# A phase of its own, with seven products of quarter matrices, for the first output product

## The chip, the cores and the metric

The kernel runs on one core of a Trainium2 chip. The metric is the device time of one execution in microseconds (us), as the median of several runs.

## The reference, cut to what matters

```python
# q, k, v: (8, 8, 576, 64); attention inside chunks of 64 tokens, per head
attn = softmax(q_c @ k_c.T / 8)                    # 64 x 64 per chunk and head
x = (attn @ v_c)  ->  (4608 tokens, 512)
h = maximum(maximum(x @ w1, x @ w2), x @ w3)       # w1..w3: 512 x 768
y = h @ w_out                                      # w_out: 768 x 512, the first output product
u = maximum(y @ w_in2, 0)                          # w_in2: 512 x 2048
out = (u * u) @ w_out2                             # w_out2: 2048 x 512
```

Weights arrive as 64-bit floats for w1 to w3, w_out, w_in2 and w_out2 (512 KB for 128x512 numbers), q, k and v as 32-bit floats.

## The kernel before, in words

The 4608 tokens are 9 blocks (NB) of 512 tokens (TB); attention goes by 36 tiles of 128 tokens. Every matrix product is done with float32r operands in three terms: each operand is kept as a high part (a cast by ACT) and a low part (the rest, a subtraction by DVE), and high x high, high x low, low x high are summed in PSUM. A matmul here is always 128x128 against 128x256.

Four stages follow each other on PE. Stage 1, up to about 160 us, is a list of tokens written out by hand (`order`, lines 642 to 658, inside `tc.manual_schedule()`): attention of tiles 0 to 7 (`qk` load, `S` scores, `M`, `X`, `N`, `G` softmax steps, `T` transposes, `E`, `V` product with v, `H`, `L` high and low part of x), the 24 units that load and convert w1 to w3 and w_out (`U` load, `A C s h l` conversion on ACT, DVE, POOL, ACT, DVE), the projections of blocks 0 and 1 (`p` + block, group f, matrix w; 24 matmuls each; `ep` is what follows on ACT or DVE, `hh` and `hl` the split of h), and the first output product of block 0 (`y`, 24 matmuls per group f). `@` is one step of the attention of later tiles, `~` a piece of its softmax. Everything after the list is placed by the framework's planner, by the program's order and its own costs; each engine's queue then runs in order.

Stage 2, blocks 2 to 8 (lines 693 to 730): 18 projections a block (`p1`), the first output product (`g2`, accumulating over six groups f in four PSUM banks, one group behind the projections), one attention step per group f, and, on ACT, DVE, POOL and the DMA queue, `park`: the 8 + 8 slices of w_in2 and w_out2 are converted, combined into seven matrices per group of four and written to DRAM as high and low part (two chains of steps, `early`, 22 steps of each chain in a block). A last output y of `g2` is copied out of PSUM and written to DRAM (`y_d`).

Stage 3 (lines 736 to 775) does y @ w_in2 with seven products of half-size matrices in place of eight (`z`; 12 matmuls per product, 9 x 4 groups), which takes three ACT copies out of PSUM and DVE sums to put together; `split_y` makes the seven combinations of y and their parts. Stage 4 (lines 776 to 790) does the last product in the same way (`g4`).

All DMAs are issued by SP, in order. SBUF slots: `w` (44) and `wz` (12) tiles of 128x512, `m` (14) operands, `in` (4), `xh` and `xl` (2 each), `t` (8) temporaries. PSUM: `acc` 4 banks, `p` 2, `at` 2.

Of the kernel before, what the change touches and what calls it, by code (L numbers as in the profile page):

```python
# [31 lines left out]
NW = 44  # L32
NZ = 12
NM = 14
NG = 4
EARLY = 48

# [4 lines left out]
def kernel(ctx: ExitStack, tc, qkv, w123, w_out, w_in2, w_out2, out):  # L42
# [21 lines left out]
    def late_tile(name):  # L64
        return wp.tile([P, 512], F32R, tag="wz", name=name, bufs=NZ)

# [5 lines left out]
    zero = const.tile([P, 512 + 64 * NZ], BF16, name="zero")[:, 0:512]  # L72
# [45 lines left out]
    def unit(src, name, keep, late):  # L118


        hi, lo = [halved(late_tile(name + n) if late else wp.tile([P, 512], F32R, tag="w", name=name + n)) for n in "hl"]
# [9 lines left out]
        def A():  # L131
            if double:
                box["r"] = wp.tile([P, 512], F32, tag="w", name="r")
                box["a"] = rounded(raw, box["r"])
# [20 lines left out]
    def combine(q, left, eng):  # L155
# [3 lines left out]
        def op(name, x, y, how):  # L159
            t = tmp(name)  # L160
            eng.tensor_tensor(out=t.rearrange("p (a c) -> p a c", a=2), in0=x, in1=y, op=how)
            return t.rearrange("p (a c) -> p a c", a=2)
# [53 lines left out]
    def fetch(n, g, i, place):  # L216
        ts = []
        for j in range(2):
            if place < NZ // 2:
                t = late_tile(f"{n}{'hl'[j]}")  # L220
            else:
                t = wp.tile([P, 512], F32R, tag="w", name=f"{n}{'hl'[j]}")
            nc.sync.dma_start(t.bitcast(F32), parked[n, g][i - 1, j])
            ts.append(halved(t))
        return ts

    def operands(wide, name, early=0):
# [12 lines left out]

    def w123_unit(f, w):
        return unit(
            w123[f, :, w * 512:(w + 1) * 512], f"w{w}_{f}", lambda *t: W123.update({(f, w): t}), w == 1
        )

    def wo_unit(f):
        return unit(w_out[f * P:(f + 1) * P, :], f"wo{f}", lambda *t: WO.update({f: t}), False)
# [133 lines left out]
    def proj(wpair, xpair, name, parts=1):  # L381

        p = ps_tile("p", name)
# [12 lines left out]

    h_t, yacc, st = {}, {}, {}
    y_d = [dp.tile([P, KD, TB], F32, name=f"yd{b}") for b in range(NB)]

    def p1_end(b, f, w, p):  # L400

        if w == 0:
            st[b] = tmp("s1")
            nc.scalar.copy(st[b], p)
        elif w == 1:
            m = tmp("m1")
            nc.vector.tensor_tensor(out=m, in0=p, in1=st[b], op=ALU.max)
            st[b] = m
        else:
            h = tmp("h")  # L410
            nc.vector.tensor_tensor(out=h, in0=p, in1=st[b], op=ALU.max)  # L411
            hh, hl = h_t[b, f] = (operand("hh"), operand("hl"))
            yield
            nc.scalar.copy(hh, h)  # L414
            yield
            nc.vector.tensor_tensor(out=hl, in0=h, in1=hh.bitcast(F32), op=ALU.subtract)
        yield

    def p1(b, f, w):
        *_, p = proj(W123[f, w], x_t[b], f"p{w}")  # L420
        run(p1_end(b, f, w, p))

    def g2(b, f):
        if f == 0:
            yacc[b] = [ps_tile("acc", f"y{d}") for d in range(KD)]
        hp = h_t.pop((b, f))
        wh, wl = WO[f]
        for d in range(KD):
            a, c = d // 2, slice(d % 2 * P, d % 2 * P + P)
            mm_k(yacc[b][d], (wh[:, a, c], wl[:, a, c]), hp, f, f == 0, f == NF1 - 1)  # L430
        if f == NF1 - 1:
            for d in range(KD):
                ys = tmp("ys")
                if d % 2:
                    nc.vector.tensor_copy(ys, yacc[b][d])
                else:
                    nc.scalar.copy(ys, yacc[b][d])
                nc.sync.dma_start(y_d[b][:, d, :], ys)
            del yacc[b]

# [12 lines left out]
    def split_y(b, parts):  # L453

        ops = y_t[b] = operands(b % 2 == 0, "y", 0 if b else EARLY)
        q = [parts[k][:, :, n * HC:n * HC + HC] for k in range(2) for n in range(2)]
        for i, x in combine(q, False, nc.vector):
            split(x, *ops[i])
# [46 lines left out]
    def split_g(parts, wide, early):  # L505
# [4 lines left out]
        for i, x in combine(q, True, nc.vector):  # L510
            split(x, *ops[i])
            yield

    def g4(g, i, ops):
# [3 lines left out]
        for m in range(2):  # L518
            t = slice(m * P, m * P + P)
            for a in range(2):  # L520
                for j, (l, r) in enumerate(((gh, wh), (gh, wl), (gl, wh))):
# [3 lines left out]
                    )  # L525

# [55 lines left out]
    units = []  # L582
    for f in range(NF1):
        units += [lambda f=f, w=w: w123_unit(f, w) for w in range(3)] + [lambda f=f: wo_unit(f)]
    units[3:7] = units[4:7] + units[3:4]
# [45 lines left out]
    def item_steps(b, f, w):  # L631

        for p in proj(W123[f, w], x_t[b], f"p{w}", 2 if (b, f, w) in split_items else 1):
            yield
# [8 lines left out]
        U1 qk0 U2 U0 qk1 qk3 qk2 qk4 qk5 v0 v1 qk7 qk6 v2 v3 A1 C1 S0 s1 U5 v4 U3 M0 v5 A2 h1 C2 A0 l1  # L643
        X0 C0 S1 M1 s0 U4 v7 U6 S3 N0 X1 S2 N1 G0 M3 G1 T0 S4 M2 X3 E0 S5 N3 X2 h0 T1 N2 V0 E1 G3 M4 V1
        G2 T3 M5 X4 S7 s2 H1 H0 T2 N4 S6 E2 L0 h2 G4 X5 L1 V2 E3 l0 T4 M7 H2 V3 E4 q000 N5 H3 A5 L3 G5
        V4 L2 C5 q001 H4 A3 T5 M6 s5 U9 v6 p000 C3 X6 A4 p001 N6 U7 ep000 X7 G6 E5 N7 T6 G7 ep001 V5 E6
        l2 h5 T7 L4 s3 H5 V6 h3 p002 l3 H6 C4 E7 h4 s4 U8 p010 ep002 A6 l4 A7 L5 L6 p011 C7 A8 l5 ep010
        U11 C6 V7 p012 H7 ep011 s6 U10 h6 L7 h7 s7 A9 p100 l6 ep012 C8 p101 C9 h8 U12 ep100 hh01 s9 A10
        p102 hl01 h9 ep101 s8 hh00 l9 A11 p110 ep102 l7 C10 A12 p111 ep110 l8 U14 C12 p020 s10 ep111 h12
        C11 p112 hl00 h11 U15 U13 s12 ep020 h10 s11 p120 ep112 l10 A14 A15 C14 p021 ep120 s14 U18 h14  # L650
        A13 l14 p022 hh11 l12 ep021 C15 p030 ep022 s15 U19 U16 hh02 h15 l11 C13 y0 h13 s13 U17 ep030
        p121 l13 A16 hl02 C16 p031 ep121 h16 s16 A17 p122 ep031 hh10 hl11 A18 A19 y1 C19 l15 p130 ep122
        C18 C17 h18 p032 ep130 s18 h17 U21 U22 U20 U23 p131 s17 s19 y2 ep131 l18 ep032 l17 p132 l16 A21
        hh03 C21 p140 ep132 h21 s21 h19 l21 p141 ep140 A20 p142 ep141 p040 ep142 C20 hl10 h20 p041 s20
        hh13 ep040 l20 A23 hl03 p042 A22 ep041 y3 ep042 l19 C23 p050 @ h23 hh04 hl04 C22 p150 ep050 ~
        s22 s23 p051 ep150 ~ h22 hh12 l22 hl12 p151 @ l23 ep051 p152 ep151 p052 @ y4 ep052 ep152 hh05
        hl05 ~ y5 hh14 hh15 hl15 hl14 hl13 ~
# [4 lines left out]
    for token in order:  # L662
# [15 lines left out]
        elif kind == "y":  # L678
            g2(0, int(n))
        else:  # L680
            b, f, w = map(int, (n + "2")[:3])
# [3 lines left out]
        if token in ("S1", "V1"):  # L685
            heat(4)
        if token == "p041":
            for load in (att_load_v, att_load):
                for t in (8, 9):
                    load(t)  # L690

    first.__exit__(None, None, None)
    for f in range(NF1):
        if f not in (1, 5):
            att.pop(0)()
            soften()
            soften()
        g2(1, f)


    early = [chain.from_iterable([park(n, g) for g in range(NG)]) for n in ("wi", "wo2")]
    late = [("wi", g, i) for g in range(NG) for i in (1, 2, 5, 6, 3, 7, 4)]
    late += [("wo2", g, i) for g in range(NG) for i in (2, 1, 5, 6, 3, 7, 4)]

    def load_late(n):
        for _ in range(n):
            if late:
                w = late.pop(0)
                (WI if w[0] == "wi" else WO2)[w[1:]] = fetch(*w, (-1 - len(late)) % (7 * NG))

    pend = None
    for b in range(2, NB):
        for f in range(NF1):
            for w in range(3):
                p1(b, f, w)
                if b < NB - 1:
                    go(*early)
                    if w == 1 and f < 4:
                        go(*early)
                if w == 1 and pend:  # L720
                    g2(*pend)
                    pend = None
# [6 lines left out]
            pend = (b, f)  # L729
            if b == NB - 1 and f == 0:  # L730
                run(split_y(0, load_y(0)))
    assert not att and not todo and [next(e, None) for e in early] == [None, None]
    while late[0][:2] <= ("wi", 1):
        load_late(1)

    groups = [(b, g) for b in range(NB) for g in range(NG)]
    last = None
    more = iter(())
    for b in range(NB):
        for g in range(NG):  # L740
# [4 lines left out]
            if pend:  # L745
                g2(*pend)
                pend = None
            if last:
                bank["at"] = last[0]
                relu2(z(*last[1], 4, "at", False), *last[1], 1, 0)  # L750
                bank["at"] = a
# [9 lines left out]
            last = (a, (b, g))  # L761
# [79 lines left out]
```

## Time and profile before

| | |
|---|---|
| median of 3 runs | 1370.91 us (1370.04 to 1372.42) |
| the profiled execution | 1374.33 us, span 1372.5 us |
| PE busy | 1355.5 us, 99%, 13697 matmuls |
| DVE, ACT, POOL busy | 66%, 38%, 14% |
| granted TensorE clock, mean | 0.998 |
| DMA | 222.33 MB, 162 GB/s on the mean |

PE is TensorE's matmuls, DVE VectorE, ACT ScalarE, POOL GpSimd, SP the engine that issues the DMAs. The duration of one matmul in the rows includes its latency and overlaps with the next; the distance from start to start is the pace. A row by windows gives, for each stretch, its length and each engine's busy time in us with the number of instructions, then the granted clock as a share of full speed, the busy share of the 16 DMA engines and what they moved.

### The profile page before, as it was taken

The numbers are of one execution on the slowest core, as the hardware profiler recorded it, in microseconds if no ns is written. First come the engines' busy times: TensorE is split into PE (matmuls) and PEld (weight loads), VectorE is DVE, ScalarE is ACT, GpSimd is POOL, SyncE is SP. The second block draws the span as 40 slices with busy tenths as digits, with TensorE's granted clock in tenths as the row PEclk, the third lists the DMA queues.
The fourth block names the chain that finished last, engine by engine and source line by source line (L and its number), as shares of the span: only waits on it lengthen the run. The fifth ranks groups of instructions, "written<-read, shape, count | busy, mean of one in ns | idle before, by whom it ended". The sixth has DMA issues, their size and how long they took to land.

```text
span 1372.5 us, 32674 instructions
## 1 busy us (share of the span) xinstructions
PE 1355.5 (99%) x13697; PEld 1342.0 (98%) x13699; DVE 900.9 (66%) x1437; ACT 519.4 (38%) x904; POOL 194.4 (14%) x180
## 2 busy tenths in 40 slices
PE   7999999999999999999999999999999999999998
PEld 5999999999999999999999999999999999999998
DVE  6874665665665565623366666667667888878774
ACT  4643333343343343311233233333334444444442
POOL 3321233222422332300000000000000000000000
PEclk9999999999999999999999999999999999999999
DMA  9442454554545644617643333343598443444341
GB/s 266 134 124 85 132 165 144 204 174 146 212 145 169 230 140 161 232 49 236 192 158 120 139 139 147 139 146 138 178 353 319 151 146 126 133 142 149 129 141 45
DMA packets 101235, 222.33 MB, mean 162 GB/s; under 512 B 11232, under 2 KB 20448, under 8 KB 101088
## 3 DMA queue, kind: packets, MB, share of 16 engines
q1 hardware_dynamic: 101088, 220.25, 48.0%
q8 instruction: 107, 1.75, 0.5%
q14 instruction: 40, 0.33, 0.1%
HBM read 134.22 MB, written 85.98 MB: 160 GB/s over the span
## 4 chain that ended last, share of the span: by engine, by line
PE 86%; DVE 1%; issue 0%; POOLq 0%; POOL 0%; ACT 0%; DVEq 0%; ACTq 0%
PE z L471 25%; PE p L376 25%; PE o L522 25%; PE y L376 9%; PE X L347 1%; PE S L286 1%; PE T L319 1%; DVE pl L212 0%; DVE u L494 0%; POOL u L494 0%; POOLq L837 0%; DVE mx L293 0%; DVE sm L305 0%; DVE e L296 0%; DVE h L411 0%
## 5 line engine op out<-in xcount | busy, mean ns | idle before, releaser
L471 PE MATMUL z<-yxh,wih 128*128 128x256 f32 x560 | 154.9, 277 | 0.0
L471 PE MATMUL z<-yxh,wil 128*128 128x256 f32 x560 | 154.7, 276 | 0.0
L471 PE MATMUL z<-yxl,wih 128*128 128x256 f32 x560 | 154.7, 276 | 0.0
L522 PE MATMUL o<-wo2h,gl 128*128 128x256 f32 x504 | 139.2, 276 | 0.0
L522 PE MATMUL o<-wo2h,gh 128*128 128x256 f32 x504 | 139.2, 276 | 0.0
L522 PE MATMUL o<-wo2l,gh 128*128 128x256 f32 x504 | 139.2, 276 | 0.0
L522 PE MATMUL o<-wo2h,gxl 128*128 128x256 f32 x504 | 139.1, 276 | 0.0
L522 PE MATMUL o<-wo2l,gxh 128*128 128x256 f32 x504 | 139.1, 276 | 0.0
L522 PE MATMUL o<-wo2h,gxh 128*128 128x256 f32 x504 | 139.1, 276 | 0.0
L494 DVE TENSOR_TENSOR c<-z,s 128x512 f32<-128x512 f32 x108 | 74.2, 687 | 78.3 <-PE z L471 74.9
L414 ACT CAST hh<-h 128x512 fp32r<-128x512 f32 x54 | 33.4, 621 | 240.6 <-DVE h L411 222.5
L471 PE MATMUL z<-yh,wih 128*128 128x256 f32 x448 | 123.6, 276 | 0.0
L471 PE MATMUL z<-yl,wih 128*128 128x256 f32 x448 | 123.6, 276 | 0.0
L471 PE MATMUL z<-yh,wil 128*128 128x256 f32 x448 | 123.6, 276 | 0.0
L411 DVE TENSOR_TENSOR h<-p,m 128x512 f32<-128x512 f32 x54 | 37.1, 689 | 131.3 <-PE p L376 131.3
L494 POOL TENSOR_TENSOR u<-u,s 128x512 f32<-128x512 f32 x9 | 12.0, 1333 | 751.7 <-DVE u L494 653.2
L479 ACT COPY s<-z 128x512 f32<-128x512 f32 x108 | 63.5, 588 | 142.2 <-PE z L471 142.2
L471 PEld LDWEIGHTS z<-yxh,wih 128*128 128x128 f32 x560 | 105.1, 188 | 0.1
L471 PEld LDWEIGHTS z<-yxl,wih 128*128 128x128 f32 x560 | 105.2, 188 | 0.0
L471 PEld LDWEIGHTS z<-yxh,wil 128*128 128x128 f32 x560 | 105.1, 188 | 0.0
L522 PEld LDWEIGHTS o<-wo2l,gxh 128*128 128x128 f32 x504 | 94.6, 188 | 0.0
L522 PEld LDWEIGHTS o<-wo2h,gxl 128*128 128x128 f32 x504 | 94.6, 188 | 0.0
(184 smaller groups left out, 4056.6 us busy)
## 6 DMA issues: line engine op xcount, KB each, us to landing
gd<-g SPq DMA_DIRECT2D x144, 256.0 KB, 2.0
gr<-gd SPq DMA_DIRECT2D x72, 512.0 KB, 4.3
qk<-in_qkv SPq DMA_DIRECT2D x28, 512.0 KB, 4.2
raw<-in_w_out SPq DMA_DIRECT2D x22, 512.0 KB, 3.8
raw<-in_w SPq DMA_DIRECT2D x18, 512.0 KB, 3.9
v<-in_qkv SPq DMA_DIRECT2D x72, 128.0 KB, 5.8
yd<-ys SPq DMA_DIRECT2D x36, 256.0 KB, 3.0
yr<-yd SPq DMA_DIRECT2D x18, 512.0 KB, 5.2
```

Of the source, the lines that this page charges most:

```text
L286: nc.tensor.matmul(s_t[t][o:o + D, h ^ t % 2, :], lhsT=q[r, h, :], rhs=k[r, h, :], start=True, stop=True,)
L319: nc.tensor.transpose(tp[:, p * P:(p + 1) * P], e[:, 2 * p:2 * p + 2, :].rearrange("p h k -> p (h k)"), ident)
L347: nc.tensor.matmul(xps_t[t][j * D:j * D + D, p, c * D:c * D + D], lhsT=v[o:o + D, c, p, :], rhs=et[o:o + D, p, q:q + D], start=True, stop= ...
L376: nc.tensor.matmul(dst[:, c], lhsT=lhs, rhs=rhs[:, c], start=first and i == 0 and j == 0, stop=last and j == len(pairs) - 1, skip_group_ch ...
L411: nc.vector.tensor_tensor(out=h, in0=p, in1=st[b], op=ALU.max)
L414: nc.scalar.copy(hh, h)
L471: nc.tensor.matmul(dst[:, a * HC:a * HC + HC], lhsT=l[:, a, w], rhs=r[:, k, :], start=first and a + k + j == 0, stop=j == 2, skip_group_ch ...
L479: nc.scalar.copy(t, bank[tag])
L494: (eng or nc.vector).tensor_tensor(out=t, in0=x, in1=y, op=ALU.add)
L522: nc.tensor.matmul(bank[i][:, m * HC:m * HC + HC], lhsT=l[:, a, t], rhs=r[:, a, :], start=g + m + a + j == 0, stop=g == NG - 1 and j == 2, ...
```

## The change

The first output product leaves stages 1 and 2 and becomes a phase between stage 2 and stage 3. h (768 features x 512 tokens) and w_out (768 x 512) are cut into quarters (384 x 256 each), and seven products of combinations of quarters replace the eight. What each part does:

- `p1_end` no longer splits h. It writes h's quarters to DRAM (`h_d`), and for every second group f forms four differences of quarters with DVE (`t`, `u`, each 128x256) and writes them too: seven matrices per block.
- `park_wo`, first in the chain of w_in2, converts w_out, combines its quarters on POOL and writes seven matrices (high and low parts, three tiles each) to DRAM. The six w_out units leave stage 1.
- `load_h`, `split_h` and `yq` are the new phase: load the seven h matrices of the next block, split them (two casts on ACT, two subtractions on DVE for each), multiply (18 matmuls per product), and put the results together with three sums on DVE and four copies on ACT, as in stage 3. `last` is product 4 of the block before; `pull` fetches one weight matrix of w_in2 (nine in blocks 0 and 1 together), two in block 8.
- Projections of stage 2 use the four `acc` banks (in stage 1 those with f > 0), the hand-written order of stage 1 is a new one, without `y`, `hh`, `hl`; `c` stands for the differences of h. 28 steps of each preparation chain go into a block. The attention steps that stood in block 1's output product (lines 693 to 698) are `@` tokens now, seven in all.
- `w` has 56 slots, `wz` is gone; stage 3 and 4 exchange which blocks use the wide operands.

```diff
 def p1_end(b, f, w, p):
@@ w == 2
-            h = tmp("h")
-            nc.vector.tensor_tensor(out=h, in0=p, in1=st[b], op=ALU.max)
-            hh, hl = h_t[b, f] = (operand("hh"), operand("hl"))
-            yield
-            nc.scalar.copy(hh, h)
-            yield
-            nc.vector.tensor_tensor(out=hl, in0=h, in1=hh.bitcast(F32), op=ALU.subtract)
+            h = weight("h", F32)
+            nc.vector.tensor_tensor(out=h, in0=p, in1=st[b, f], op=ALU.max)
+            h = halved(h)
+            j = f // 2
+            if f % 2 == 0:
+                nc.sync.dma_start(h_d[b][0, :, j, :], h[:, 0, :])
+                h_t[b, j] = h
+            else:
+                nc.sync.dma_start(h_d[b][1:5:3, :, j, :].rearrange("i p n -> p i n"), h)
+                yield
+                q = h_t.pop((b, j))
+                t, u = [halved(weight(n, F32)) for n in "tu"]
+                for out, x, y in (
+                    (t[:, 0], q[:, 1], q[:, 0]), (t[:, 1], h[:, 1], t[:, 0]),
+                    (u[:, 0], h[:, 1], q[:, 1]), (u[:, 1], h[:, 0], t[:, 1]),
+                ):
+                    nc.vector.tensor_tensor(out=out, in0=x, in1=y, op=ALU.subtract)
+                for k, x in ((2, t), (5, u)):
+                    nc.sync.dma_start(h_d[b][k:k + 2, :, j, :].rearrange("i p n -> p i n"), x)
...
-    def g2(b, f):
...
+    def load_h(b, part):
+        if part == 0:
+            pairs, one = ((0,) if b == 0 else (0, 2)), ((2, 3, 4, 5) if b == 0 else ())
+        else:
+            pairs, one = (), ((6,) if b == 0 else (4, 5, 6))
...
+    def split_h(b):
+        for k, i in enumerate(QN):
+            if i in (3, 4):
+                t = ap.tile([P, KD, TB], F32R, tag="xl", name=f"h{i}").rearrange("p k n -> p (k n)")
...
+            else:
+                ts = [operand("h" + n) for n in "hlm"]
...
+            for h, y in zip(hi, xs):
+                nc.scalar.copy(h, y)
+            for h, l, y in zip(hi, lo, xs):
+                nc.vector.tensor_tensor(out=l, in0=y, in1=h.bitcast(F32), op=ALU.subtract)
+            yield
+    def yq(b, i, tag, first):
...
+        for a in range(2):
+            c = slice(a * P, a * P + P)
+            for j in range(NJ):
+                for k, (l, r) in enumerate(((wh, hh), (wh, hl), (wl, hh))):
+                    nc.tensor.matmul(
+                        dst[:, a * HC:a * HC + HC], lhsT=l[j][:, c], rhs=r[j],
+                        start=first and a + j + k == 0, stop=k == 2, skip_group_check=True,
+                    )
...
@@ order, its last lines
+        l11 h13 U16 U15 C14 U17 p122 ep121 s14 s13 p130 s12 A16 h12 C16 p031 l12 h16 s16 h14 ep130 p131
+        A15 ep031 l13 ep122 l14 p032 C15 h15 s15 A17 p040 C17 ep131 p041 s17 ep040 ep032 h17 c01 p132
+        ep041 l17 l15 p042 ep132 c11 l16 p050 @ ep042 p051 ~ ~ ep050 p052 @ @ ep051 p140 ~ ep052 c02
+        p141 @ ep140 p142 ~ ep141 p150 @ @ p151 ~ ep150 p152 @ ~ ep151 ep142 ep152 c12
...
-    for f in range(NF1):
-        if f not in (1, 5):
-            att.pop(0)()
...
-        g2(1, f)
...
-    early = [chain.from_iterable([park(n, g) for g in range(NG)]) for n in ("wi", "wo2")]
+    early = [
+        chain(park_wo(), *[park("wi", g) for g in range(NG)]), chain(*[park("wo2", g) for g in range(NG)])
+    ]
...
                 if b < NB - 1:
                     go(*early)
-                    if w == 1 and f < 4:
+                    if w and f < 5:
                         go(*early)
...
+            if b == NB - 1:
+                if f == 0:
+                    load_h(0, 0)
+                    more = split_h(0)
+                else:
+                    next(more)
...
+    for b in range(NB):
+        if b + 1 < NB:
+            load_h(b + 1, 0)
+        yq(b, 1, "at", True)
+        a, s1 = bank["at"], take("at", "s1")
+        next(more)
+        pull(b)
+        c11 = plus(yq(b, 2, "p", True), s1, "c11")
+        put_y(b, 0, 0, c11)
+        if last:
+            last()
+        bank["at"] = a
+        next(more)
+        pull(b)
+        if b + 1 < NB:
+            load_h(b + 1, 1)
+            more = split_h(b + 1)
+        else:
+            more = split_y(0, load_y(0))
+        yq(b, 5, "acc", True)
+        s5 = take("acc", "s5")
+        next(more)
+        pull(b)
+        yq(b, 6, "at", False)
...
```

## Rows read from the trace of the kernel before

**Rows 1.** Page: busy us, share of the span, instructions.
```profile
PE 1355.5 (99%) x13697; PEld 1342.0 (98%) x13699; DVE 900.9 (66%) x1437; ACT 519.4 (38%) x904; POOL 194.4 (14%) x180
```
**Rows 2.** Windows: stretch, its length, each engine's busy us, clock, DMA share, GB/s.
```profile
0.00:10.00 10.00, 5.18 (x43) 2.42 (x43) 3.92 (x8) 3.96 (x6) 1.97 (x7) 1.00 0.79 278
10.00:20.00 10.00, 8.04 (x170) 6.78 (x172) 9.32 (x19) 3.81 (x8) 3.36 (x3) 0.83 1.06 301
20.00:30.00 10.00, 7.24 (x125) 5.60 (x125) 8.45 (x18) 3.52 (x7) 4.36 (x4) 0.83 1.06 239
...
60.00:80.00 20.00, 20.00 (x179) 20.00 (x178) 16.61 (x26) 11.14 (x20) 7.58 (x5) 1.00 0.43 132
```
**Rows 3.** Timeline of PE: start, us, instructions, [idle before, releaser].
```profile
11.31 1.97 PE L286 MATMUL S<-k,q 64*64 64x64 f32 x32 [4.25 <-DMA k<-in_qkv]
...
23.84 1.27 PE L347 MATMUL X<-et,v 64*64 64x64 f32 x32 [2.42 <-issue]
...
37.81 0.39 PE L376 MATMUL p<-xh,w_0h 128*128 128x256 f32 x1 [1.31 <-issue]
...
88.47 0.39 PE L376 MATMUL y<-hh,wo0h 128*128 128x256 f32 x2
```
**Rows 4.** Windows in stages 3 and 4.
```profile
700.00:900.00 200.00, 200.00 (x1766) 200.00 (x1765) 132.63 (x205) 69.88 (x121) 0.00 (x0) 1.00 0.38 138
...
1100.00:1300.00 200.00, 200.00 (x1768) 200.00 (x1767) 164.75 (x261) 92.94 (x158) 14.28 (x11) 1.00 0.42 139
```
**Rows 5.** Windows, only instructions that touch tiles y (PE, PEld, DVE, ACT).
```profile
0.00:1373.00 1373.00, 156.48 (x1296) 151.27 (x1296) 12.35 (x18) 10.56 (x18) 1.00 0.49 162
```
**Rows 6.** Windows, block 3 of stage 2.
```profile
251.80:323.00 71.20, 71.20 (x841) 70.42 (x840) 45.67 (x72) 28.03 (x50) 19.77 (x20) 1.00 0.54 179
```
**Rows 7.** Groups by line (busy us, mean ns): whole run, 320:400, 480:560, 160:240.
```profile
L416 DVE TENSOR_TENSOR hl<-h,hh 128x512 fp32r<-128x512 f32 x54 | 44.0, 818 | 23.0 <-ACT hh L414 22.8
L411 DVE TENSOR_TENSOR h<-p,m 128x512 f32<-128x512 f32 x54 | 37.1, 689 | 131.3 <-PE p L376 131.3
L414 ACT CAST hh<-h 128x512 fp32r<-128x512 f32 x54 | 33.4, 621 | 240.6 <-DVE h L411 222.5
L479 ACT COPY s<-z 128x512 f32<-128x512 f32 x108 | 63.5, 588 | 142.2 <-PE z L471 142.2
L212 DVE TENSOR_TENSOR pl<-q,ph 128x512 fp32r<-128x512 f32 x24 | 19.1, 821 | 7.6 <-ACT ph L210 4.5 <-DMA wi0d<-pl 2.2 <-DMA wo21d<-ph 0.9
...
L416 DVE TENSOR_TENSOR hl<-h,hh 128x512 fp32r<-128x512 f32 x7 | 7.0, 1003 | 3.6 <-ACT hh L414 3.6
...
L212 DVE TENSOR_TENSOR pl<-s,ph 128x512 fp32r<-128x512 f32 x2 | 3.5, 1774 | 0.0
...
L308 DVE TENSOR_SCALAR sm<-sm 128x8 f32<-128x8 f32 x8 | 1.7, 223 | 0.0
```
**Rows 8.** Windows around the step from stage 3 to stage 4.
```profile
990.00:1000.00 10.00, 10.00 (x90) 10.00 (x90) 5.23 (x8) 2.36 (x4) 0.00 (x0) 1.00 0.98 334
...
1010.00:1020.00 10.00, 10.00 (x91) 10.00 (x90) 8.30 (x14) 4.18 (x8) 0.00 (x0) 1.00 0.99 344
1020.00:1030.00 10.00, 10.00 (x88) 9.90 (x87) 7.86 (x13) 4.93 (x9) 0.00 (x0) 1.00 0.99 355
...
1040.00:1050.00 10.00, 10.00 (x91) 10.00 (x90) 8.22 (x14) 4.67 (x8) 0.00 (x0) 1.00 1.04 390
...
1070.00:1080.00 10.00, 10.00 (x90) 10.00 (x90) 9.89 (x17) 4.18 (x8) 0.00 (x0) 1.00 0.64 200
```
**Rows 9.** Timelines of PE, ACT and DVE before block 2.
```profile
175.53 1.16 PE L347 MATMUL X<-et,v 64*64 64x64 f32 x64
...
182.19 0.39 PE L376 MATMUL p<-xh,w_0h 128*128 128x256 f32 x2
...
176.73 1.08 ACT L357 CAST xh<-X 128x512 fp32r<-128x512 f32 x2 [0.81 <-PE X L347]
...
177.35 1.29 DVE L362 TENSOR_TENSOR xl<-X,xh 128x512 fp32r<-128x512 f32 x2 [0.20 <-ACT xh L357]
```
**Rows 10.** Page: DMA issues, KB each, median us from issue to landing.
```profile
yr<-yd SPq DMA_DIRECT2D x18, 512.0 KB, 5.2
```

More of the change, by code (lines that the diff above doesn't have):

```diff
@@ L36 @@
 EARLY = 48
+NJ = NF1 // 2
+FO = [f for j in range(NJ) for f in (j, NJ + j)]
+QN = (1, 2, 5, 6, 3, 7, 4)
 E_INF, E_ZERO = 122880.0, 2.0**-15
@@ L116, in convert, with unit @@
             nc.gpsimd.tensor_tensor(out=part.bitcast(U32), in0=au[:, c], in1=ru[:, c], op=ALU.add)
-    def unit(src, name, keep, late):
-        hi, lo = [halved(late_tile(name + n) if late else wp.tile([P, 512], F32R, tag="w", name=name + n)) for n in "hl"]
+    def unit(src, name, keep):
+        hi, lo = [halved(weight(name + n)) for n in "hl"]
         keep(hi, lo)
@@ new lines, in operands, with split_into @@
+    def operands(wide, name, early=0):
+        if not wide:
+            return {}
+        ts = [[ap.tile([P, KD, TB], F32R, tag=t, name=f"{name}{t}{i}") for i in range(2)] for t in ("xh", "xl")]
+        ops = {i: [halved(ts[j][i // 4][:, i % 4, :]) for j in range(2)] for i in range(1, 8)}
+        if early:
+            ops[1] = [
+                halved(t[0].rearrange("p k n -> p (k n)")[:, TB - early:2 * TB - early]) for t in ts
+            ]
+        return ops
+    def split_into(ops, i, x, name):
+        if i not in ops:
+            ops[i] = [halved(operand(name + n)) for n in "hl"]
+        split(x, *ops[i])
@@ L417, in p1_end @@
         yield
     def p1(b, f, w):
-        *_, p = proj(W123[f, w], x_t[b], f"p{w}")
+        *_, p = proj(W123[f, w], x_t[b], f"p{w}", tag="acc")
         run(p1_end(b, f, w, p))
-    def g2(b, f):
[L424 to L439, printed above, removed]
@@ L707, in load_late @@
             if late:
-                w = late.pop(0)
-                (WI if w[0] == "wi" else WO2)[w[1:]] = fetch(*w, (-1 - len(late)) % (7 * NG))
-    pend = None
+                kind, g, i = late.pop(0)
+                if kind == "wi1":
+                    WQ[i] = fetch(kind, g, i)
+                else:
+                    (WI if kind == "wi2" else WO2)[g, i] = fetch(kind[:2] if kind == "wi2" else kind, g, i)
+    more = iter(())
     for b in range(2, NB):
@@ L728, with pull, last @@
                     load_late(1)
-            pend = (b, f)
-            if b == NB - 1 and f == 0:
-                run(split_y(0, load_y(0)))
-    assert not att and not todo and [next(e, None) for e in early] == [None, None]
-    while late[0][:2] <= ("wi", 1):
-        load_late(1)
+            if b == NB - 1:
[4 more added lines that the diff above has]
+                    next(more)
+    assert not att and not todo and [next(e, None) for e in early] == [None, None]
+    def pull(b):
+        load_late(2 if b == NB - 1 else int(len(late) > 39))
+    load_h(0, 1)
+    last = None
+    for b in range(NB):
+        bank["at"] = None
+        if b + 1 < NB:
[14 more added lines that the diff above has]
+            more = split_h(b + 1)
+        else:
+            more = split_y(0, load_y(0))
[4 more added lines that the diff above has]
+        yq(b, 6, "at", False)
+        s2 = take("at", "s2")
+        next(more)
+        pull(b)
+        put_y(b, 0, 1, plus(yq(b, 3, "acc", False), s2, "c12"))
+        next(more)
+        put_y(b, 1, 1, plus(yq(b, 7, "at", False), s5, "c22"))
+        next(more)
+        next(more)
+        pull(b)
+        def last(a=a, b=b):
+            bank["at"] = a
+            yq(b, 4, "at", False)
+            put_y(b, 1, 0, take("at", "c21"))
     groups = [(b, g) for b in range(NB) for g in range(NG)]
-    last = None
-    more = iter(())
+    run(more)
     for b in range(NB):
```

210 lines of the change are left out of this document (121 added, 89 removed).

## The prediction

> **What bounds the kernel now.** Read the busy shares first: PE is busy 99% of the span, DVE 66% [rows 1]. Then read PE's time stage by stage, because a busy share hides idle starts and matmul latency. In the first 40 us PE is short of input: the DMA engines are full, the granted clock averages 0.83 from 10 to 30 us (a part of it at 1.2 GHz instead of 2.4), and the PE timeline shows waits for k and for issue [rows 2, 3]. From 60 us on PE has no idle time that matters [rows 2, 4]: 1766 matmuls in 200 us is 113.25 ns per 128x256 matmul [rows 4], and this is 256 columns at 2.4 GHz plus a few ns, at a granted clock of 1.00. So after the start the time is a count of matmuls. DVE at 82% of 200 us (row 1100:1300) and DMA engines at 0.98 to 1.04 from 990 to 1050 us do not slow PE: it does 88 to 91 matmuls in every 10 us there [rows 4, 8].
>
> **The term the change is made for.** The first output product (tiles y) is 1296 matmuls [rows 5]: 9 blocks x 6 x 4 x 6. The new product of quarters takes per block 7 products x 2 x 3 x 3 = 126 instead of 144, so 9 x 18 = 162 matmuls go. 162 x 113.25 ns = 18.3 us. All of it is on the path, since PE is the path. The new matmuls change weights every time, as those of the second layer (row 700:900) do already; so the pitch stays. Low end of the gain: 0 if something else takes over; high end: 18.3 us.
>
> **The start.** The six loads and conversions of w_out leave the early queue (6 x 512 KB and the work of ACT, DVE and POOL on each) and the weights of the second group come two units sooner; on the other side the first output product of blocks 0 and 1, 2 x 144 x 113 ns = 33 us of PE work that could fill holes, leaves too. Before, PE was idle 4.25, 2.42 and 1.31 us at the points of rows 3; none of it is filled by y, whose first matmul is at 88 us. The units per PE time stay alike (18 units for 98 us of projections against 24 for 131 us, 5.4 us each). The new order loads q and k of tiles 0 and 1 ahead of any weight, so the 4.25 us hole may shrink, but one more transpose and one more V product stand ahead of the first projection. The DMA engines' load of 278, 301 and 239 GB/s for 30 us [rows 2] sets when the eight tiles are in, and this I don't see changing. Bounds: -4 (the hole goes) to +4 us (it comes back elsewhere); I take 0.
>
> **The passage into block 2.** Before, outputs of tiles 10 and 11 (X at 175.53) are followed by two y groups; ACT's cast of X ran 176.73 to 177.81 and DVE's subtraction ended at 178.64, while PE worked on y until 182.2 [rows 9]. Afterwards the last of the seven attention steps stands behind the last projection of block 1, and next on PE is block 2's first projection, which reads those very columns. The cover is gone: X ends at 176.69 in the old times and the last low half at 178.64, so PE waits some 2 us, less two or three matmuls that read columns already there. Tile 9's transpose also comes only two projections (5.4 us) behind its scores, against some 6 us of DVE operations at 0.65 us each [rows 9] and POOL's product: 0.3 us, an estimate. I take +2.3 us (0 to 4).
>
> **Blocks 2 to 7.** A block takes 71.2 us now, with 45.67 us of DVE, 19.77 of POOL and 179 GB/s, so 12.7 MB [rows 6]. Without y (144 x 113 ns = 16.3 us) it takes 54.9 us, and the other engines get no such relief. DVE: the six hl subtractions go (6 x 818 ns = 4.9 us), two ys copies go (1.4), and twelve 128x256 subtractions for the sums of h come (t, u). No row shows one; a 128x8 operation costs 0.2 us and a 128x512 one 0.69 [rows 7], so 0.2 to 0.69 each; I take 0.44, nearest to half of the larger plus the fixed part: 5.3 us. The weight preparation steps run 28 times a block in each of two chains where they ran 22 times. Their DVE share now is 45.7 less projections (12 x 0.69), hl, ys and four tiles of attention (12.3): about 19 us; times 28/22 this is 5.1 us more, w_out's own conversion included. Sum: 49.8 us in 54.9, 91%. It lasts 4.3 blocks, until the w_out2 chain of 120 steps is done. DMA: 12.7 - 1 (y) + 2.75 (h) + 2.1 (denser preparation) = 16.5 MB in 54.9 us, 301 GB/s. Both are under what rows 8 show beside a full PE (DMA up to 390 GB/s; DVE at 9.89 of 10 us with 90 matmuls). ACT loses the hh casts and has room. PE has four accumulator banks instead of two for projections, so a late maximum costs nothing until it is three projections (8 us) late. What can hurt is a transpose that waits for the chain DVE, ACT, DVE, POOL in full queues; it has about 16 us for about 7 us of work. I take +2 us (0 to 16).
>
> Here a rule of the Trainium skill speaks against the change. First the rows: the hl subtraction, with both inputs in SBUF, takes 818 ns on the mean and 1003 in the window 320:400, while h, with one input in PSUM, stays at 689 [rows 7]; so beside POOL such an operation has lost 0.13 us on the mean, 1.6 us for the twelve new ones, and the 91% become 94%. "SBUF — State Buffer", section "Who interferes with whom", says that a VectorE instruction with two SBUF inputs and a GpSimd instruction that reads SBUF shut each other out for the whole instruction. By that rule every one of the twelve that meets a POOL operation would wait for its end; with POOL at some 45% of the shorter block and half of a POOL operation (19.77 us / 20 = 0.99 us [rows 6]) left to wait for, that is an estimated 2.7 us a block and 96%. By neither does DVE pass PE; what it would do if it did is rival (a), worked out there from rows.
>
> **The new phase.** Per block 126 x 113.25 ns = 14.3 us of PE. ACT: 7 x (0.62 + about 0.4) + 4 x 0.59 = 9.5 us; DVE: 7 x (0.69 + 0.44) + 3 x 0.69 = 10.0 us; both hidden, and each product (2.04 us) is longer than that of the second layer (1.36 us), which runs the same pattern of banks without idle time [rows 4]; a cast takes 0.62, a copy from PSUM 0.59, a maximum or sum 0.69 us [rows 7]. DMA: reads of 2.75 MB and writes of 1.05 MB per block, 266 GB/s; while block 0 and 1 also fetch nine 512 KB weights it is about 430 GB/s, above the 344 to 390 of rows 8. But a load is issued at the head of the block before and its first split comes four products (8.2 us) later; a 512 KB read of y took 5.2 us from issue to landing [rows 10], a 786 KB one by that 6 to 8. The surplus of blocks 0 and 1 is 2 x 1 MB, about 6 us of queue, against a lead of half a block. Taken at 0 (0 to 8). Into the second layer: y of block 0 is split before the phase ends, and product 4 of the last block is put behind the first two z products. 0.
>
> **Sum.** -18.3 + 0 + 2.3 + 2 + 0 = -14.0 us. The profiled execution took 1374.33 us (span 1372.5), so 1360.3 in its own terms; it lies 3.4 us above the median of 1370.91, and against the median the sum gives 1356.9 us. I forecast 1357.
>
> **Rivals.**
> (a) Blocks 2 to 6 fall to DVE and POOL, a little: DVE's 91% with longer instructions beside POOL passes 100% for stretches. For it: 91% is above the 82% that held for 200 us. Against: the full 10 us of rows 8. If DVE needs 57 us a block, 2.1 x 4.3 = 9 us more: about 1364, up to 1370.
> (b) The same place, far over: the pl subtractions run at the 1774 ns that one window shows instead of their mean (821 ns for the plainest) [rows 7]; 56 steps of 30 a preparation make 13 of them a block, 12.4 us more, so DVE needs 62.2 us, 7.3 more than PE's 54.9, over 4.3 blocks 31 us: 1357 + 31 - 2 = 1386, slower. It decides from DVE = 58.6 us a block, where 3.7 x 4.3 eats the 16 us that are left of the gain. For it: POOL's share of a block rises from 28% [rows 6] to about 45%. Against: waits lengthen POOL's side as well, so lock time is not added twice.
> (c) The new phase waits for h: if each of the nine blocks is late by 1 us, or blocks 0 to 2 by 3, 1366. For it: 430 GB/s asked. Against: the lead of 8 us, then 266 GB/s.
> (d) The start gains: q and k first take away the 4.25 us hole, nothing is lost in blocks 2 to 7: 1351.
> (e) PE does not get shorter, because the 33 us of y taken out of the first 180 us were filler there: only if idle times of rows 3 reappear between 60 and 150 us. Against: PE idle there was nil with two more units per block to prepare. In (a)'s range.
>
> **How the numbers follow.** Forecast (1352 to 1362) 0.55; (a) and (e) 0.16; (b) 0.09; (c) 0.09; (d) 0.11. A measurement of this kernel can't tell less than about 0.2% (2.7 us) from no change. Faster: forecast, (d), (c) and most of (a), less a little for what no row shows: 0.81. Same: 0.08, the top of (a). Slower: (b) and a remainder, 0.11. The likeliest case alone reaches from 1352 to 1362; the range from 1349 to 1369 takes in (d), (c) and most of (a).
>
> **What would show it.** Right: 1134 matmuls in the new phase, in 128 to 131 us; PE full from 60 us to the end but for one wait of about 2 us for xl before block 2; DVE near 90% in blocks 2 to 5; DMA mean near 205 GB/s. Wrong: idle PE waiting for POOL e or for a projection's bank in blocks 2 to 6 (a, b); ACT copies waiting for the h loads with PE behind them (c); a first projection much before or after 33 us (d); matmuls of the new phase slower than 113 ns.

## The result: slower by 0.6%, and the profile after

The changed kernel takes 1378.8 us (median of 19 runs, 1374.5 to 1391.0) against 1371.9 us before: ratio 1.0056, 95% interval 1.0043 to 1.0069. I had forecast 1357, in a range of 1349 to 1369. The runs also spread more than those of the kernel before (1370.0 to 1373.3). The profiled execution took 1379.76 us, span 1378.0.

The page, to be read against [rows 1]: PE has 162 matmuls less and 10 us less busy time, and the span is 5.5 us longer; DVE is up 82 us and the DMA moves 282.94 MB at 205 GB/s.

```profile
PE 1345.2 (98%) x13535; PEld 1330.0 (97%) x13537; DVE 982.9 (71%) x1634; ACT 549.4 (40%) x1002; POOL 210.7 (15%) x194
...
DMA packets 146617, 282.94 MB, mean 205 GB/s; under 512 B 14368, under 2 KB 56992, under 8 KB 146464
```

The starts of the stages on PE show where the time went. "Blocks 2 to 8" before is counted without its y matmuls (7 x 144 x 113.25 ns = 114.2 us). The first matmul of block 2 starts at 182.19 us before and at 147.32 us after; the waits of the passage into block 2 stand behind it, so they count in the second row.

| stretch on PE | before | after | difference | forecast |
|---|---|---|---|---|
| start to first projection of block 2 | 182.2 | 147.3 | -34.9 | -32.6 (y of blocks 0 and 1) |
| blocks 2 to 8, without y | 384.3 | 409.0 | +24.7 | +4.3 (passage 2.3, blocks 2) |
| y of blocks 2 to 8 / the new phase | 114.2 | 128.6 | +14.4 | +14.2 |
| rest | 691.8 | 693.1 | +1.3 | 0 |
| span | 1372.5 | 1378.0 | +5.5 | -14 |

Nearly the whole loss is in the second row. Windows of the kernel after, about one for each of blocks 2, 3, 5 and the new phase (stretch, its length, busy us of PE, PEld, DVE, ACT, POOL, clock, DMA share, GB/s), to be read against [rows 6]:

```profile
148.50:212.50 64.00, 58.82 (x703) 57.26 (x704) 51.89 (x92) 23.99 (x43) 26.36 (x28) 0.97 0.63 209
212.50:272.00 59.50, 56.92 (x696) 55.74 (x695) 52.89 (x92) 28.84 (x56) 32.58 (x31) 0.97 0.92 312
...
332.00:392.00 60.00, 56.73 (x693) 55.85 (x694) 49.01 (x86) 26.23 (x48) 28.23 (x27) 0.97 0.87 290
```
```profile
556.00:684.00 128.00, 128.00 (x1131) 128.00 (x1130) 79.67 (x151) 70.66 (x152) 0.00 (x0) 1.00 0.90 313
```

From head to head blocks 2, 3 and 5 take 65.2, 60.7 and 61.6 us where 54.9 were expected. DVE is at 81 to 89% there (91 was forecast), and yet PE has idle time and a mean clock of 0.97. The new phase has PE full, 1131 matmuls recorded in 128 us, with the DMA engines at 0.90. The idle places, from PE's timeline (start, us, instructions, [idle before, releaser]); the first row is a pair of scores that is needed further down:

```profile
189.93 1.16 PE L331 MATMUL S<-qk 64*64 64x64 f32 x64
...
203.67 0.33 PE L392 MATMUL X<-et,v 64*64 64x64 f32 x4 [3.02 <-issue]
...
214.50 0.39 PE L421 MATMUL p<-xh,w_0h 128*128 128x256 f32 x1 [1.71 <-ACT xh L402]
215.87 0.58 PE L421 MATMUL p<-xl,w_0h 128*128 128x256 f32 x1 [0.87 <-DVE xl L407]
...
335.17 0.56 PE L421 MATMUL p<-xl,w_0h 128*128 128x256 f32 x1 [3.31 <-DVE xl L407]
...
395.26 0.39 PE L421 MATMUL p<-xl,w_0h 128*128 128x256 f32 x1 [1.81 <-DVE xl L407]
```

Most are at the heads of blocks, where the first projection reads the parts of x that DVE and ACT have just made. All idle places between the start of block 2 and the new phase sum to 15.3 us. Behind some of them PE runs at the lower clock level, 1.2 GHz, for a while:

```profile
200.00:220.00 20.00, 14.13 (x143) 13.38 (x142) 19.58 (x30) 8.11 (x16) 12.37 (x11) 0.83 0.85 297
320.00:340.00 20.00, 15.31 (x167) 14.77 (x168) 18.12 (x33) 7.63 (x15) 11.51 (x12) 0.91 0.74 252
380.00:400.00 20.00, 18.09 (x195) 17.59 (x194) 18.45 (x31) 8.38 (x15) 10.11 (x11) 0.92 0.74 246
```

A mean clock of 0.83 over 20 us is 3.4 us of full clock lost (0.17 x 20); the three windows lose 6.8 us. Idle and clock are 22.1 of the 24.7 us; the rest isn't accounted for.

Why PE waits there: DVE is late, and it is late because it has waited in line itself. Timeline of ACT, DVE and POOL around the wait at 203.67:

```profile
194.59 0.67 ACT L93 ACTIVATE a<-raw 128x512 f32<-128x512 f32 x1 [3.10 <-DMA raw<-in_w_out]
...
203.60 1.23 ACT L344 ACTIVATE e<-e 128x512 f32<-128x512 f32 x2 [7.31 <-DVE e L341]
```
```profile
195.29 0.43 DVE L101 TENSOR_SCALAR a<-a 128x512 f32<-128x512 f32 x1 [2.48 <-ACT a L93]
...
196.82 0.68 DVE L457 TENSOR_TENSOR h<-p,m 128x512 f32<-128x512 f32 x1
197.42 0.63 DVE L472 TENSOR_TENSOR t<-h 128x256 f32<-128x256 f32 x1
197.98 0.96 DVE L472 TENSOR_TENSOR u<-h 128x256 f32<-128x256 f32 x1
198.86 1.51 DVE L472 TENSOR_TENSOR t<-h,t 128x256 f32<-128x256 f32 x1
200.40 1.37 DVE L472 TENSOR_TENSOR u<-h,t 128x256 f32<-128x256 f32 x1
201.70 1.28 DVE L338 TENSOR_REDUCE mx<-S 128x8 f32<-128x512 f32 x2
202.90 1.27 DVE L341 TENSOR_TENSOR e<-S,mx 128x512 f32<-128x512 f32 x2
```
```profile
206.46 2.37 POOL L358 TENSOR_TENSOR e<-e,rs 128x512 f32<-128x512 f32 x2 [4.97 <-ACT ph L211]
```

Scores that PE finished at 191 us are reduced from 201.70 on: ahead of them stand a conversion whose raw tile landed late, and the four t and u operations, 4.3 us in one piece. The scores fill both `at` banks until the subtraction `e<-S,mx` (202.90 to 204.17) has read them, and the V product of the tiles before needs these banks. The profile names no releaser for the wait at 203.67; the program's order and these times say that it was this one. Over the stretch 148:460 (engine, line, what it waited for: us in total, times, longest):

```profile
ACT a L93 <- DMA raw<-in_w_out: 29.2, 9, 7.0
ACT a L93 <- DMA raw<-in_w_in: 13.2, 6, 4.1
```
```profile
DVE a L101 <- ACT a L93: 30.7, 12, 5.5
DVE m L453 <- PE p L421: 10.3, 4, 4.2
```

Before, from 182 to 610 us, ACT came 2 times to a raw tile that hadn't landed, and DVE waited 120 us for projections: it was ahead of PE. Afterwards ACT came 15 times to one in 312 us, and DVE is behind.

```profile
ACT a L91 <- DMA raw<-in_w_in: 2.9, 2, 1.5
```
```profile
DVE h L411 <- PE p L376: 87.5, 30, 4.7
DVE m L407 <- PE p L376: 33.0, 20, 5.7
```

### The profile page after: what moved, and what is told of

Same layout as the page of the kernel before. It is cut to its first block, busy times and chain, and to the rows that moved or that the text cites. A ratio compares the mean times of both kernels' runs of the same rounds, so it can differ in the third digit from the quotient of the medians.

```text
span 1378.0 us, 33127 instructions
## 1 busy us (share of the span) xinstructions
PE 1345.2 (98%) x13535; PEld 1330.0 (97%) x13537; DVE 982.9 (71%) x1634; ACT 549.4 (40%) x1002; POOL 210.7 (15%) x194
## 2 busy tenths in 40 slices
DMA packets 146617, 282.94 MB, mean 205 GB/s; under 512 B 14368, under 2 KB 56992, under 8 KB 146464
## 4 chain that ended last, share of the span: by engine, by line
PE 82%; DVE 7%; DMA 5%; issue 2%; ACT 1%; POOL 1%; SPq 1%; POOLq 0%; DVEq 0%; ACTq 0%
PE o L561 25%; PE z L510 24%; PE p L421 22%; PE y L614 9%; DMA raw<-in_w_out 2%; PE S L331 1%; DVE a L103 1%; PE T L364 1%; PE X L392 1%; DVE a L106 1%; DVE pl L213 1%; DVE xl L407 1%; DVE t L472 1%; DVE mx L338 1%; DVE sm L350 1%
## 5 line engine op out<-in xcount | busy, mean ns | idle before, releaser
L510 PE MATMUL z<-yh,wih 128*128 128x256 f32 x560 | 154.8, 276 | 1.4 <-ACT s L518 1.3
L510 PE MATMUL z<-yl,wih 128*128 128x256 f32 x560 | 154.6, 276 | 0.0
L510 PE MATMUL z<-yh,wil 128*128 128x256 f32 x560 | 154.6, 276 | 0.0
L510 PE MATMUL z<-yxh,wih 128*128 128x256 f32 x448 | 123.8, 276 | 0.0
L510 PE MATMUL z<-yxh,wil 128*128 128x256 f32 x448 | 123.7, 276 | 0.0
L510 PEld LDWEIGHTS z<-yh,wih 128*128 128x128 f32 x560 | 105.1, 188 | 1.8 <-ACT s L518 1.5
L510 PEld LDWEIGHTS z<-yh,wil 128*128 128x128 f32 x560 | 105.1, 188 | 0.0
L510 PEld LDWEIGHTS z<-yl,wih 128*128 128x128 f32 x560 | 105.1, 188 | 0.0
L561 PEld LDWEIGHTS o<-wo2h,gxh 128*128 128x128 f32 x504 | 94.6, 188 | 0.0
L561 PEld LDWEIGHTS o<-wo2h,gh 128*128 128x128 f32 x504 | 94.6, 188 | 0.0
```

What stands on the lines that cost most here:

```text
L510: nc.tensor.matmul(dst[:, a * HC:a * HC + HC], lhsT=l[:, a, w], rhs=r[:, k, :], start=first and a + k + j == 0, stop=j == 2, skip_group_ch ...
L561: nc.tensor.matmul(bank[i][:, m * HC:m * HC + HC], lhsT=l[:, a, t], rhs=r[:, a, :], start=g + m + a + j == 0, stop=g == NG - 1 and j == 2, ...
```

## The experiments

Each ratio is to the kernel before, timed beside it. The edits are to the changed kernel unless said otherwise. The expectations set two explanations against each other above all. Theory C says that DVE and POOL have more work than a block has time. Theory W says that ACT and DVE stand in line behind raw loads that land late. L, B and T name the parts of x, the PSUM banks and the t and u operations.

**Attention one step ahead.**
```diff
-                if att and w == 0:
+                if att and (w == 0 or (b, f, w) == (2, 1, 2)):
```
Expected: 

> One attention step more is done in block 2 (group 1), so every later one comes one group f (about 9 us) earlier; nothing else is changed. Theory L (late x): the about 20 us lost in stage 2 are PE waits for the parts of x at the heads of blocks, because DVE and ACT run some us behind, and the half clock behind these waits; with 9 us of lead they go: 1358 to 1364, granted clock 1.00 in blocks 3 to 6. Theory C (capacity): DVE has more work than a block has time; the wait then only moves to another place: 1374 or more.

Measured: 1380.3 us, ratio 1.006 (1.0041 to 1.008). Theory L falls, and the time is what theory C gave: the wait only moved. PE's waits leave the heads of the blocks and turn up at transposes, which wait for the PSUM bank of the X before, until DVE has read it for xl:

```profile
176.98 1.30 PE L364 MATMUL T<-ident,e 128*128 128x128 f32 x5 [4.46 <-DVE xl L407]
```

**A thinner chain for w_out2.**
```diff
                     if w and f < 5:
-                        go(*early)
+                        go(early[0])
+                    if w == 1 and f < 3:
+                        go(early[1])
```
Expected: 

> The chain that prepares w_out2 goes by 21 steps a block instead of 28 (120 steps in 5.7 blocks instead of 4.3); the other chain stays at 28. Theory C (DVE and POOL too full): DVE falls from 88% to about 82% in blocks 2 to 5, and 8 to 15 us of the 20 lost come back: 1364 to 1371. Theory W (ACT and DVE wait in line for raw loads that land late): fewer loads per us, a smaller gain, 1370 to 1375.

Measured: 1368.5 us, 0.9975 (0.9961 to 0.9989): 10 us come back, as theory C gave. But DVE's busy time in 148:460 stays (255.5 against 256.9 us, since PE advances faster), so it is not the fall in DVE's share that theory C named; ACT's waits for raw loads fell from 42.4 to 20.4 us.

**Conversions that don't wait for their load.**
```diff
+    raw0 = const.tile([P, 512, 2], U32, name="raw0")
+    nc.sync.dma_start(raw0.rearrange("p n w -> p (n w)"), w_out[0:P, :].bitcast(U32))
...
-                    for k, _ in enumerate(convert(raw, parts)):
+                    for k, _ in enumerate(convert(raw0, parts)):
```
Expected: 

> The conversions of w_in2, w_out2 and w_out in stage 2 read one tile that was loaded once, so the prepared weights are those of one slice; all raw loads are still done and no one reads them. Two of eight temporary slots are given up for it. Work and DMA traffic are as before, only ACT's wait for a raw load is gone. Theory W: ACT's 42 us and DVE's 31 us of waiting in line go and with them most of the 20 us: 1358 to 1365. Theory C: 1373 to 1379.

Measured: 1366.6 us, 0.9957 (0.9945 to 0.9969). 12 us of 20 come back. That is nearer to theory W than to C, but 1.6 us above W's range: a wait of 3.3 us at the head of block 3 is left. DVE was busy 270.2 us in 148:460, more than in the changed kernel, while PE waited less.

**No sums of h.**
```diff
-                t, u = [halved(weight(n, F32)) for n in "tu"]
-                for out, x, y in (
...
-                    nc.vector.tensor_tensor(out=out, in0=x, in1=y, op=ALU.subtract)
-                for k, x in ((2, t), (5, u)):
+                for k, x in ((2, q), (5, h)):
```
Expected: 

> The twelve 128x256 subtractions of a block that form the sums of h are left out, plain quarters are written in their place (same bytes). They took 0.54 to 0.81 us each, 8.2 us a block. Theory T (these bursts beside POOL, 3 to 4 us in one piece ahead of the softmax, are what makes the attention late): 1360 to 1366. Theory W: they only move the queue a little, 1370 to 1377.

Measured: 1366.4 us, 0.9957 (0.9945 to 0.997). Also 12 us, just above theory T's range. Taking DVE work out of the line helps as much as taking the waits out. ACT's waits for raw loads fell with it, from 42.4 to 28.0 us, with the same loads; so the two gains overlap and can't be added.

**No preparation of w_out2 at all.**
```diff
+    early[1] = iter(())
...
-                    (WI if kind == "wi2" else WO2)[g, i] = fetch(kind[:2] if kind == "wi2" else kind, g, i)
+                    (WI if kind == "wi2" else WO2)[g, i] = fetch("wi", g, i)
```
Expected: 

> The whole chain that prepares w_out2 is left out (the last product then reads the matrices of w_in2; 16 of 38 raw loads and their DVE, ACT, POOL work and writes go). If everything that is lost lies in the density of stage 2, this is what the change is worth on PE alone: 1355 to 1360, PE idle in stage 2 under 3 us. If part is lost for other reasons (clock, the new phase), 1363 or more.

Measured: 1357.8 us, 0.9895 (0.9875 to 0.9915). PE's waits from 148 us to the new phase:

```profile
PE p L421 <- ACT xh L402: 0.8, 1, 0.8
PE T L364 <- POOL e L358: 0.7, 1, 0.7
PE p L421 <- DVE xl L407: 0.3, 1, 0.3
```

So nothing but the preparation packed into stage 2 stands between the change and its count of matmuls, and the passage into block 2 costs 1.8 us. Whether the steps cost by their work or by their waits this run can't tell, since both went.

**Conversion three steps behind the load, in one step.**
```diff
                     yield
-                    for k, _ in enumerate(convert(raw, parts)):
-                        if k in (0, 2):
-                            yield
+                    yield
+                    yield
+                    run(convert(raw, parts))
                     yield
```
Expected: 

> The same work, the same number of steps and the same loads; only the order is changed: the conversion of a raw tile stands three steps (about 5 us) behind its load instead of one, and is then done in one step. Theory W (waits in line for loads): ACT's 42 us of waiting for raw falls below 15, 5 to 12 us come back: 1366 to 1374. Theory C (DVE and POOL capacity): 1376 to 1381.

Measured: 1371.3 us, 0.9999 (0.998 to 1.0018). 7.5 us come back with the same work and loads; ACT's wait for raw falls from 42.4 to 13.9 us. By capacity alone nothing should have moved.

```profile
ACT a L93 <- DMA raw<-in_w_out: 10.8, 6, 3.5
ACT a L93 <- DMA raw<-in_w_in: 3.1, 2, 1.6
```

**V products in the idle p banks, attention one step ahead.**
```diff
-            att_V(t, t + 1)
+            att_V(t, t + 1, tag="p")
```
Expected: 

> As the run with attention one step ahead (1380), and the V products of stage 2 go to the two p banks, which the change left idle there, so that a transpose no longer waits for the bank of a late xl. Theory B (the two at banks tie PE to DVE's lag): PE's waits for xl (10 us with the half clock behind them) go, 1360 to 1370. Theory C: no better than 1375.

Measured: 1386.1 us, 1.0093 (1.0074 to 1.0112). Theory B falls, and the time is again what theory C gave: with the attention let loose, the projections' maxima come later in DVE's line and PE waits for their banks.

```profile
244.75 0.50 PE L421 MATMUL p<-xh,w_3h 128*128 128x256 f32 x2 [3.23 <-DVE h L457]
...
267.45 0.80 PE L421 MATMUL p<-xh,w_4h 128*128 128x256 f32 x2 [6.13 <-DVE m L453]
```

**All four edits** (ahead, p banks, thinner chain, later conversion). Expected: 

> All four: w_out2's chain at 21 steps a block, conversion three steps behind the load, attention one step ahead, V products in the p banks. Nothing is left out. By theories W and B together nearly all of the 20 us come back: 1356 to 1362, under the kernel before by 0.7 to 1.2%. By theory C alone only the thinner chain counts: 1366 to 1370.

Measured: 1361.1 us, 0.9912 (0.9895 to 0.9928). ACT still waited 21.4 us for raw loads in 148:460, and PE lost next to nothing by it; such a wait doesn't cost PE time by itself.

**Thinner chain and later conversion only** (the two diffs above, together). Expected: 

> Two of the four edits of the combined kernel (1361): w_out2's chain at 21 steps a block and conversion three steps behind its load; attention and banks as after the change. If density and lateness of loads are the cause and attention one step ahead with the p banks adds nothing (it lost 1 to 7 us when it was tried alone), this is 1358 to 1364. If the lead of the attention is needed too, 1365 to 1370.

Measured: 1357.4 us (1356.6 to 1360.0), 0.9897 (0.9883 to 0.9912). It leaves nothing out and beats both kernels. Its windows (the last two rows set the stretch 148:460 of the changed kernel against its own), and what ACT waited for raw in 148:460:

```profile
200.00:260.00 60.00, 58.68 (x726) 57.50 (x725) 53.18 (x85) 27.62 (x53) 31.43 (x30) 1.00 0.82 272
260.00:320.00 60.00, 60.00 (x742) 59.23 (x741) 53.53 (x87) 22.47 (x40) 28.81 (x26) 1.00 0.86 285
...
148.00:460.00 312.00, 296.96 (x3584) 291.05 (x3585) 256.88 (x433) 128.53 (x236) 139.32 (x132) 0.98 0.79 266
148.00:460.00 312.00, 309.98 (x3886) 305.08 (x3886) 266.07 (x452) 132.80 (x242) 145.89 (x139) 1.00 0.82 271
```
```profile
ACT a L93 <- DMA raw<-in_w_out: 4.5, 2, 3.3
ACT a L93 <- DMA raw<-in_w_in: 3.8, 2, 2.5
```

DVE is at 89% for 120 us, as full as in the changed kernel's worst block, while PE is idle 1.3 us in the first 60 us and full in the second. Over 148:460 DVE, ACT, POOL and the DMA engines all do more than in the changed kernel, and PE is busy 13 us longer. A busy share of 89% was therefore not the bound.

**h not written in blocks 2 to 7.**
```diff
-                nc.sync.dma_start(h_d[b][1:5:3, :, j, :].rearrange("i p n -> p i n"), h)
+                if not 2 <= b <= 7:
+                    nc.sync.dma_start(h_d[b][1:5:3, :, j, :].rearrange("i p n -> p i n"), h)
...
-            nc.sync.dma_start(t, h_d[b][k])
+            nc.sync.dma_start(t, h_d[1 if 2 <= b <= 7 else b][k])
```
Expected: 

> The writes of h and its differences to DRAM are left out for blocks 2 to 7 (the new phase reads those of block 1 there): 2.75 MB of 16.5 less in a block, 50 of 290 GB/s, and twelve issues of SP; DVE's subtractions stay. Theory W (raw loads land late because the DMA engines are nearly full): raw lands in about 4 us instead of 5.2, ACT's 42 us of waiting for it halve, 5 to 12 us come back: 1367 to 1374. Theory C: 1376 to 1380.

Measured: 1369.5 us, 0.9978 (0.9967 to 0.9989). 9 us; raw loads of this stretch land in 4.7 and 4.3 us instead of 5.2 and 5.1, ACT waits 29.9 us for them, where half of 42 was expected. The time is in theory W's range, but issue slots of SP went as well and were not told apart. That rival has some ground: in the changed kernel's SP line, which is in order, the write of h of every second group waited 32.0 us for DVE in 148:460 (12 times, up to 10.8 us), and at four of these places a raw load was among the next four issues.

**The kernel before, dense.**
```diff
                     go(*early)
-                    if w == 1 and f < 4:
+                    go(*early)
+                    if w == 1:
                         go(*early)
```
Expected: 

> The kernel before with one number changed: 42 steps of each preparation chain in a block instead of 22. Its block of 71 us then has 0.59 steps per us and chain, the changed kernel's of 55 us has 0.51. If density alone makes the loss, without quarters of h, t, u, or h's writes: the chains end after 2.9 blocks, DVE is near 88% there, and 8 to 20 us are lost: 1380 to 1392. If the new work of the change is needed for it, at most 1375.

Measured: 1387.5 us, 1.0116 (1.0099 to 1.0133): one number of the old kernel makes a loss of 15 us, without the new phase or any of its work (its steps are planned denser than the changed kernel's, 0.59 against 0.51 per us). In 182:395 it looks like this; then what ACT waited for raw in 160:420, and what PE waited for in 160:620:

```profile
182.00:395.00 213.00, 202.43 (x2338) 199.19 (x2338) 174.81 (x262) 104.72 (x186) 110.26 (x104) 0.99 0.73 249
```
```profile
ACT a L91 <- DMA raw<-in_w_in: 18.5, 6, 4.3
ACT a L91 <- DMA raw<-in_w_out: 2.5, 4, 1.0
```
```profile
PE p L376 <- DVE h L411: 5.7, 6, 1.6
PE p L376 <- DVE m L407: 5.2, 3, 3.5
```

DVE is at 82% here on the mean of 213 us, below the 89% over 120 us of the kernel that loses nothing. PE waits in another place than in the changed kernel: not for parts of x, but for projections' maxima, which are late in DVE's line.

**The same, conversion three steps behind the load** (the two more `yield`s of above, put into the kernel before). Expected: 

> The dense kernel before (1387.5 at 42 steps a block) with the conversion three steps behind its raw load. If waits in line for loads are what turns density into lost time, also without the new phase, the 15 us lost shrink by a third or more: 1374 to 1382, and ACT's 21 us of waiting for raw fall below 8. If DVE's and POOL's capacity is what counts there, 1385 to 1389.

Measured: 1383.5 us, 1.0073 (1.0053 to 1.0092). A miss for both theories: 4 of 15 us come back, and ACT's waits for raw stay (20.5 us). At this density three steps are no cure; here the loss is not shown to be the loads.

## Why the prediction was wrong, point by point

- **The term the change is made for** (-18.3): right. The new phase took 128.6 us for 1134 matmuls (128.4 at 113.25 ns), and the kernels without the crowd come out at 1357.4 and 1357.8.
- **The start** (0): right as far as the first projection, at 33.15 us, before at 33.23; q and k first did not take the hole away, a wait of 4.49 us for k stands at 17 us instead of 11, so rival (d) falls. Up to block 2 another 2.3 us were gained beyond y's matmuls (-34.9 against -32.6), which the sum put at 0 and no run takes apart. Rival (e) didn't come: PE was idle 1.5 us from 60 to 148 us.
- **The passage into block 2** (+2.3): right, waits of 0.85, 0.34 and 0.69 us, 1.9 us.
- **Blocks 2 to 7** (+2, 0 to 16): this is the step that failed; it measured +22.8 (24.7 less the passage). The loads in it were about right: DVE 52.89 of 59.5 us in block 3 (89% where I worked out 91), DMA 312 GB/s (301). Three terms were off. A block before is 72.3 us from head to head (251.76 to 324.06); my 71.2 cut its end off, so 56.0 and not 54.9 us were left without y. t and u took 0.54 to 0.81 us each over the stretch, not 0.44, 8.2 us a block instead of 5.3. And a raw load landed in 5.2 us instead of 3.7. But the error is the inference, "both are under what rows 8 show beside a full PE". In rows 8 nothing on DVE's line waits for a raw load; in stage 2 the same line holds conversions that wait for ACT, ACT's wait for raw loads, and behind them the softmax, xl and the maxima that PE needs. When the steps went from 0.31 per us (22 in 71 us) to about 0.47 (28 in 60), ACT came 15 times in 38 loads to a tile that hadn't landed, where it had been 2 in 32, and DVE went from waiting for PE to being waited for. The slack was wrong too. I gave the chain DVE, ACT, DVE, POOL 16 us for about 7 us of work and looked for the danger at the transposes; from the scores at 191.09 us to the end of POOL's product at 208.83 us it took 17.7 us, and it was the V product that met it, at the bank of the scores. The sign that I named, PE waiting for POOL e or for a projection's bank, was therefore not the one: that was 0.7 and 1.3 us, against 8.9 us for xh and xl and 3.6 us at the V products.
- **Rival (a)** named the place and the sign, and sized it at 9 us because it counted busy time only. **Rival (b)** gave the right side by a wrong mechanism, so its 1386 is near by luck: the pl operations had 1.23 us at the worst group over the stretch, not 1.77, and DVE did not pass 100%.
- **The Trainium skill's rule** ("SBUF — State Buffer", "Who interferes with whom") asked for more than the row: 12 operations at 0.44 and 2.7 us of blocking are 8.0 us a block, 8.2 were measured; the mean of hl gave 5.3 + 1.6 = 6.9. Here the rule's estimate was the nearer one. The trace agrees in kind: of the 64 operations in 148:460 the 34 that met no POOL operation took 0.42 us on the mean, the 30 that met one 0.98 us.
- **The new phase** (0): right up to +1.3 us at its end, a first z product waiting 1.34 us for an ACT copy. Rival (c) didn't come, with the DMA engines at 0.90.

What the runs settle: the loss lies in stage 2 alone and comes from the density of the preparation steps (1357.8 without one chain, 1387.5 in the kernel before made dense), and DVE's busy share is not the bound (the thinner chain with the later conversion does more in the same 312 us and loses nothing). Late raw loads at the head of ACT's line carry a part of it: 12 us go when nothing waits for them, 7.5 when they are given three steps. DVE's extra work and the thinner chain buy about as much; that each does so by letting the lag run down is an argument, not a measurement. What stays open: how the 20 us divide between the waits for loads, late issue in SP's line and the waits for POOL (the changed kernel's ACT also waited 27.7 us for POOL's sums and conversions in 148:460, and no run takes those out), since the gains overlap; and why the later conversion leaves ACT's waits as they are in the dense kernel before.

## What to carry to other kernels

A busy share says little about an engine whose line holds waits: a line at 89% for 120 us cost PE 1.3 us, and one at 82% over 213 us went with a loss of 15 us. When a change takes time out of the bounding engine, list what the other engines must now do in the shorter stretch, and ask of each instruction in their lines what it waits for and who stands behind it. Compare a load's lead with the time that it takes at the new traffic before counting its consumer as hidden; more lead gave back 7.5 us in the changed kernel, 4 in the denser one before.

## What the runs showed of the hardware

The granted clock fell behind idle places of 1.7 to 3.3 us in stage 2: behind the 3.02 us at 203.67 (0.53 in 205.4:209, with PE busy throughout), the 1.71 and 0.87 us at 214.50 and 215.87, the 3.31 us at 335.17 and the 1.81 us at 395.26. In the kernel with the thinner chain and later conversion, whose longest wait in stage 2 is 1.0 us, it is 1.00 over 148:460.

```profile
205.40:209.00 3.60, 3.60 (x19) 3.60 (x19) 3.60 (x9) 2.42 (x6) 2.37 (x2) 0.53 0.98 381
```

So 15.3 us of idle time brought 6.8 us of lost clock with it. And the same 128x256 subtraction took 0.42 us with POOL idle and 0.63 to 1.51 us beside POOL at 197 to 201 us; the groups are those of 148:460:

```profile
153.62 0.42 DVE L472 TENSOR_TENSOR t<-h 128x256 f32<-128x256 f32 x1
...
L472 DVE TENSOR_TENSOR u<-h 128x256 f32<-128x256 f32 x16 | 12.9, 807 | 0.0
L472 DVE TENSOR_TENSOR t<-h,t 128x256 f32<-128x256 f32 x16 | 12.6, 790 | 0.0
L472 DVE TENSOR_TENSOR t<-h 128x256 f32<-128x256 f32 x16 | 9.5, 592 | 0.0
L472 DVE TENSOR_TENSOR u<-h,t 128x256 f32<-128x256 f32 x16 | 8.6, 540 | 0.2
```
